# Decode attention beside a gated Mish layer: V and its weights in one load, w1 in K's rows, another closing

## The chip, the cores and the metric

The kernel runs on one core of a Trainium2 chip. The metric is the device time of one execution in microseconds; the kernel before took 220.31 us, the median of 3 runs (220.21 to 220.89). Everything is float32.

## The reference

Two tokens (B = 2, one per batch element) go through two branches, which a gate mixes: attention over the last 4096 positions of a cache, with 32 query heads on 8 key heads, and a dense layer with Mish between two matrices.

```
g = sigmoid((x * gate_w).sum(-1, keepdims=True))          # x: 2 x 1 x 512
q = (x @ wq)                                              # 32 heads of 128
k, v = k_cache[:, :, Sk - W:, :], v_cache[:, :, Sk - W:, :]   # 8 heads, W = 4096, each used by 4 query heads
a = softmax(q k^T * Dh ** -0.5) v @ wo                    # 4096 -> 512
h = x @ w1 + b1                                           # 512 -> 1792
b = (h * tanh(softplus(h))) @ w2                          # 1792 -> 512
out = g * a + (1 - g) * b
```

## The kernel before

The program makes eight turns, one for each key head. In a turn it scores the queries of that head (both batch elements) against 4096 keys each, takes the softmax, multiplies with V, and adds the part of `wo` that belongs to the head before. Beside it, seven of the turns do two of the 14 blocks of 128 rows of the dense layer: `w1`'s pair is multiplied on VectorE, the Mish is worked out on GpSimd and ScalarE, and the result is multiplied with `w2`'s pair one turn later. Both branches add up in one PSUM tile, `acc`. The last head's part of `wo` is added behind the loop, in the tile `fin`.

**Memory.** There is one slot for K and one for V, with no second buffer. `kslot` holds K of a head (8192 numbers in each of 128 partitions) and behind it the next turn's piece of `wq` (2048). `vslot` holds V (8192), `w2`'s pair (1024) and `wo`'s part (2048). `w1s` (L48) holds all seven pairs of `w1`, 1024 numbers each, and a row of zeros for the eighth turn; one load fills it at the start. The host lays out all the arrays so that each partition's row is contiguous.

**The order of the loads.** All loads are issued by SyncE in one queue, in the order of L111 to L140. Ahead of each stands a wait for what frees the slot. K's next load (L120) waits for `qz`, which VectorE gives with the copy of the next queries (L288), behind the maximum of the scores (L329). That copy comes behind the eight products with `wq` (L325), which read the same slot. V is loaded in two halves: the first (L126) waits for `sV`, given when PE has done half of the products with V (L244); the second (L133, with `w2` and `wo` in its rows) waits for `sP`, given behind PE's last product of a turn (L260). The last turn's K, V and weights come in smaller pieces (L123, L135 to L140), so that the work at the end can follow them closely.

**PE in a turn** (L224 to L262): scores (L233), transposition of the maximum (L239), sum of the exponentials (L240), products with V (L244), `w2`'s products with the Mish of the turn before (L253), the transposition of the head's output (L257, which waits for `osel`, the end of a chain on VectorE from L342 to L344), `wo`'s products with the output of the turn before (L260), then `sP`.

**VectorE in a turn** (L322 to L348): the products with `wq` (L325), the maximum (L329), the queries' copy (L288), the bias (L333), the transposition of the probabilities (L335), the copy of `w1`'s pair into `w1c` (L336), products and sums of the dense layer (L292, L298), then the selection of the output (L342 to L344) and its copy into `wst2` (L347).

**The closing** (L264 to L280, L351 to L355): `fin` is filled by five steps of `last`, four with `wo`'s blocks and one that folds `acc`. A step multiplies a 128x32 block with two halves of 256 columns; steps named 0 write the PSUM partitions 0 to 63, those named 1 write 64 to 127. ScalarE copies the upper half to `fs` (L220), VectorE adds the lower half to it (L351), and four rows of 256 numbers are stored (L355).

Of the kernel before, what the change touches and what calls it, by code (L numbers as in the profile page):

```python
# [30 lines left out]
L = 16  # L31

AHEAD = L * (HKV - 1)
NP = PAIRS - 1


def decode_kernel(nc, xg, wq0, w1, kw, k7a, k7b, k7c, va, vb0, vb, v7b, v7c, w26, wo6, wo7a, wo7b, wo7c, out):
    T, V, A, G, SP = nc.tensor, nc.vector, nc.scalar, nc.gpsimd, nc.sync

    def sb(name, n, p=P):  # L40
        return nc.alloc_sbuf_tensor(name, [p, n], F32).ap()

    def ps(name, n):
        return nc.alloc_psum_tensor(name, [P, n], F32).ap()

    kslot = sb("kslot", CHUNK + WQH)
    ks, wqs = kslot[:, :CHUNK], kslot[:, CHUNK:]
    w1s = sb("w1s", HKV * W1P)  # L48
    w1c = sb("w1c", W1P)
    vslot = sb("vslot", CHUNK + 2 * D + WQH + 2 * HKV)  # L50
    vs, w2s, wos = vslot[:, :CHUNK], vslot[:, CHUNK : CHUNK + 2 * D], vslot[:, CHUNK + 2 * D : CHUNK + 2 * D + WQH]
# [6 lines left out]
    b16, qz, wst, hst = (zeros[:, sum(widths[:i]) : sum(widths[: i + 1])] for i in range(len(widths)))  # L58
# [4 lines left out]
    fold = sb("fold", Q)  # L63
# [24 lines left out]
    pq = sb("pq", 8)  # L88
# [2 lines left out]
    md = sb("md", 4)  # L91
    mr = sb("mr", 4)
    accs = sb("accs", D)
    fs = sb("fs", 256, 64)
    res = sb("res", 256, 64)

    acc = ps("acc", D)
    sc = ps("sc", 512)
# [3 lines left out]
    fin = ps("fin", 512)  # L102
    lp = small[:, 0:1]
    ol = small[:, 8:16]

    names = ("ld_x ld_q ld_k ld_kb ld_kc ld_v ld_vb ld_vc ld_w ld_h ld_o ld_w0 ld_w1 ld_w2 c_id c_m c_z c_xb c_eg c_g c_mg "
             "gx g0 g1 g2 g3 g4 g5 hs vx q8 rcp os1 os2 os3 qz mx sA sB bias ex pT sC osel sD sP sE sV wst pq mkr w1c w1p hx hq hd hr accs pe fs res st").split()
    sem = {n: nc.alloc_semaphore(n) for n in names}


# [3 lines left out]
    h = CHUNK // 4  # L114
    parts = ((0, 2 * h), (2 * h, 3 * h), (3 * h, 4 * h))
    for i in range(HKV):
        if i:
            SP.wait_ge(sem["qz"], i + 1)
        if i < PAIRS:
            SP.dma_start(kslot, kw[i]).then_inc(sem["ld_k"], L)  # L120
        else:
            for n, (f, t), src in zip(("ld_k", "ld_kb", "ld_kc"), parts, (k7a, k7b, k7c)):
                SP.dma_start(ks[:, f:t], src).then_inc(sem[n], L)  # L123
        if i:
            SP.wait_ge(sem["sV"], i)
        SP.dma_start(vs[:, : 2 * h], va[i]).then_inc(sem["ld_v"], L)  # L126
        if i:
            SP.wait_ge(sem["sP"], i)
        if i == 0:
            SP.dma_start(vs[:, 2 * h :], vb0).then_inc(sem["ld_vb"], L)  # L130
            SP.dma_start(w1s[:, : PAIRS * W1P], w1).then_inc(sem["ld_w"], L)
        elif i < PAIRS:
            SP.dma_start(vslot[:, 2 * h : CHUNK + 2 * D + WQH], vb[i - 1]).then_inc(sem["ld_vb"], L)  # L133
        else:
            SP.dma_start(vs[:, 2 * h : 3 * h], v7b).then_inc(sem["ld_vb"], L)  # L135
            SP.dma_start(vs[:, 3 * h :], v7c).then_inc(sem["ld_vc"], L)
            SP.dma_start(w2s, w26).then_inc(sem["ld_h"], L)  # L137
# [16 lines left out]
    G.memset(zeros, 0.0).then_inc(sem["c_z"], 1)  # L154
    G.memset(wst2, 0.0)
    G.memset(w2s, 0.0).then_inc(sem["hs"], 1)
    G.memset(w1s[:, PAIRS * W1P :], 0.0).then_inc(sem["ld_w"], L)
    G.wait_ge(sem["c_id"], 1)
    done(G.tensor_tensor(f2, ident[:, : 2 * Q], ident[:, 2 * Q :], op=ALU.add))
    done(G.tensor_tensor(fold, f2[:, :Q], f2[:, Q:], op=ALU.add))  # L160
# [6 lines left out]
    for n in range(NH):  # L167
        i = G.tensor_copy(same.rearrange("p (j y n h) -> p j y n h", j=NJ, n=NH, h=REP)[:, :, :, n, :],
                          key.rearrange("p (y h) -> p y h", h=REP)[:, None].to_broadcast([P, NJ, 4, REP]))
# [35 lines left out]
                        omg[:, None, :].to_broadcast([P, 2, B]), op=ALU.mult).then_inc(sem["hs"], 1)  # L205


    for n in ("ld_kb", "ld_kc", "ld_vc", "ld_o", "ld_h"):
        A.sem_inc(sem[n], AHEAD)
    A.wait_ge(sem["c_eg"], 1)  # L210
    A.activation(eg, zg, AF.Exp, scale=-1.0).then_inc(sem["c_eg"], 1)
# [4 lines left out]
        A.activation(pq, pq, AF.Exp).then_inc(sem["hq"], 1)  # L216
    A.wait_ge(sem["sP"], HKV)
    A.copy(accs, acc).then_inc(sem["accs"], 1)
    A.wait_ge(sem["pe"], 1)
    A.copy(fs, fin[64:, :256]).then_inc(sem["fs"], 1)  # L220


    key_rhs = same[:, :16].rearrange("p (b n h) -> p b n h", b=B, n=NH)[:, :, 0, :]
    with T.Fori(1, HKV + 1, 1) as r:  # L224
        loads = T.lower_val(r * L)

        def after(i, name):
            return i.wait_op(sem[name], loads if name.startswith("ld_") else T.lower_val(r), "sem-ge")

        T.wait_ge(sem["ld_k"], loads)  # L230
        for m in range(BN):
            for j in range(NJ):
                i = T.matmul(sc[Q * j : Q * j + Q, :], qz[:, m * Q : m * Q + Q],  # L233
                             ks[:, (m * NJ + j) * 512 : (m * NJ + j + 1) * 512],
                             start=(m == 0), stop=(m == BN - 1))
                if j == 0 and m != 1:
                    after(i, ("qz", "", "ld_kb", "ld_kc")[m])
        i.then_inc(sem["sA"], 1)
        after(T.transpose(mb[:, :P], mx.to_broadcast([P, P]), ident), "mx").then_inc(sem["sB"], 1)  # L239
        after(T.matmul(lp, same, lsum, start=True, stop=True), "ex").then_inc(sem["sC"], 1)  # L240
        T.wait_ge(sem["ld_v"], loads)
        for c in range(NC):
            j = c % NJ
            i = T.matmul(o[Q * j : Q * j + Q, :], pT[:, c * Q : c * Q + Q], vs[:, c * 512 : c * 512 + 512],  # L244
                         start=(c < NJ), stop=(c >= NC - NJ))
            if j == 0 and c != NJ:
                after(i, ("pT", "", "ld_vb", "ld_vc")[c // NJ])
            if c == NC // 2 - 1:
                i.then_inc(sem["sV"], 1)
        i.then_inc(sem["sD"], 1)  # L250
        T.wait_ge(sem["ld_h"], loads)
        for j in range(2):
            i = T.matmul(acc[Q * j : Q * j + Q, :], hst[:, j * Q : j * Q + Q], w2s[:, j * D : j * D + D],  # L253
                         start=False, stop=False, skip_group_check=True)
            if j == 0:
                after(i, "hs")
        after(T.matmul(ol, osel, key_rhs, start=True, stop=True), "osel").then_inc(sem["sE"], 1)  # L257
        T.wait_ge(sem["ld_o"], loads)
        for j in range(REP):
            i = T.matmul(acc[Q * j : Q * j + Q, :], wst[:, j * Q : j * Q + Q], wos[:, j * D : j * D + D],  # L260
                         start=False, stop=False, skip_group_check=True)
        i.then_inc(sem["sP"], 1)  # L262

    def last(s, lhs, rhs, wait=None, **kw):  # L264
        for u in range(2):
            a = Q * (2 * s + u)
            i = T.matmul(fin[a : a + Q, :256], lhs, rhs[:, u * 256 : u * 256 + 256], skip_group_check=True, **kw)  # L267
# [48 lines left out]
    with V.Fori(1, HKV + 1, 1) as r:  # L316
# [6 lines left out]
        for h in range(REP):  # L323
            for b in range(B):
                i = V.tensor_tensor_reduce(out=junk[:, (h * B + b) * D : (h * B + b) * D + D], in0=wqs[:, h * D : h * D + D],  # L325
                                           in1=xb[b], op0=ALU.mult, op1=ALU.add, scale=1.0, scalar=0.0,
                                           accum_out=q8[:, b * REP + h : b * REP + h + 1])
        i.then_inc(sem["q8"], 1)
        after(V.tensor_reduce(mx, sc, axis=AX.X, op=ALU.max), "sA").then_inc(sem["mx"], 1)  # L329
        after(queries_out(), "q8")  # L330
        V.wait_ge(sem["c_m"], 1)
# [1 line left out]
        V.tensor_tensor_reduce(out=junkb, in0=mb[:, :P], in1=mask, op0=ALU.add, op1=ALU.min, scale=-SCALE,  # L333
                               scalar=BIG, accum_out=bias).then_inc(sem["bias"], 1)
        after(V.transpose(pT, prob), "ex").then_inc(sem["pT"], 1)  # L335
        at(V.tensor_copy(w1c, w1s[:, bass.ds((r - 1) * W1P, W1P)]), "ld_w", 2 * L).then_inc(sem["w1c"], 1)  # L336
# [10 lines left out]
        after(V.tensor_copy(wst2v, ol.rearrange("p (b h) -> p h b", b=B)), "sE").then_inc(sem["wst"], 1)  # L347
# [3 lines left out]
    at(V.tensor_tensor(res, fin[:64, :256], fs, op=ALU.add), "pe", 2).then_inc(sem["res"], 1)  # L351
# [3 lines left out]
    SP.dma_start(out, res[:: Q // B, :]).then_inc(sem["st"], L)  # L355
    SP.wait_ge(sem["hs"], HKV + 1)
    SP.wait_ge(sem["st"], L)
    nums = sorted(s.num for s in sem.values())
# [46 lines left out]
```

## Time and profile before

| what | value |
|---|---|
| median of 3 runs | 220.31 us (220.21 to 220.89) |
| the profiled execution, its own time | 220.1 us |
| its span, first to last instruction | 218.8 us |
| busy: PE, VectorE, ScalarE, GpSimd | 118.8, 126.2, 10.3, 26.2 us |
| bytes read from HBM | 91.26 MB |
| mean granted clock of TensorE | 0.797 |

The profile is that of one execution. Engines are PE (matmul), PEld (its weight loads), DVE (VectorE), ACT (ScalarE), POOL (GpSimd) and SP (SyncE); SPq is SP's queue of DMA issues. Rows of the sequence views give the start in us from the span's start, the duration in us, the engine, the line, the operation and, in brackets, the idle time before it and what ended it. Rows of groups end with the busy us and the mean ns of one, then the idle time before them. In the list of DMA issues, the last number is the time from issue to landing, the median where there are several. In the chain of waits a DMA's row begins at its issue and ends when it has landed.

### The profile page before, as it was taken

The page shows a single profiled execution, that of the slowest core. Times are in us where ns is not written, and L with a number is a line of the kernel's source. Part 1 is how long each engine was busy: PE and PEld are TensorE (multiplying, and loading weights), DVE is VectorE, ACT ScalarE, POOL GpSimd, SP SyncE. Part 2 cuts the span into 40 slices and gives each one's busy share as a digit, 9 for nine tenths or more (in the row PEclk, how much of TensorE's full clock was granted, in tenths as well). Part 3 has the DMA queues.
Part 4 walks back from the last instruction along what each step waited for, and adds up shares of the span by engine and source line. Part 5 has one row for each costly group of instructions (what it writes and reads, how often), then busy time and mean ns, then how long its engine had stood idle before and what let it go on. Part 6 is the DMA issues. An engine that isn't in the chain of part 4 may idle for free.

```text
span 218.8 us, 1985 instructions
## 1 busy us (share of the span) xinstructions
PE 118.8 (54%) x668; PEld 31.1 (14%) x668; DVE 126.2 (58%) x268; ACT 10.3 (5%) x28; POOL 26.2 (12%) x118
## 2 busy tenths in 40 slices
PE   0006386058463477807547195924648175984775
PEld 0002021012110112202111022101112022120211
DVE  2897913919743468507673177714693075967850
ACT  2000010000100001000100001000100001000101
POOL 8200000220021000310012000210002100050030
PEclk9999958757969675875988757695996958599599
DMA  8898999989999999989999899999999899999993
GB/s 310 367 479 371 453 446 407 479 377 429 451 434 442 401 437 455 464 374 452 435 407 479 377 429 446 439 442 401 437 455 464 374 446 440 392 412 442 412 410 118
DMA packets 4926, 91.29 MB, mean 417 GB/s; under 512 B 552, under 2 KB 572, under 8 KB 1084
## 3 DMA queue, kind: packets, MB, share of 16 engines
q1 hardware_dynamic: 4924, 91.26, 97.8%
q8 instruction: 1, 0.02, 0.0%
q14 instruction: 1, 0.01, 0.0%
HBM read 91.26 MB, written 0.00 MB: 417 GB/s over the span
## 4 chain that ended last, share of the span: by engine, by line
DMA 73%; PE 15%; DVE 8%; SPq 2%; issue 1%; DVEq 0%
DMA vslot<-in_vb 51%; DMA w1s<-in_w 15%; PE o L244 9%; DMA wol<-in_wo7a 8%; PE acc L260 4%; DVE osc L344 3%; PE small L257 1%; DVE osc L342 1%; DVE junk L292 1%; DVE hxt L298 1%; PE fin L267 1%; SPq L113 0%; DVE w1c L336 0%; DVE xs L300 0%; SPq L137 0%
## 5 line engine op out<-in xcount | busy, mean ns | idle before, releaser
L233 PE MATMUL sc<-kslot,zeros 128*32 128x512 f32 x256 | 42.7, 823 | 51.5 <-DMA kslot<-in_kw 50.2
L325 DVE CUSTOM_DVE_ANT_0 junk<-kslot,xs 128x512 f32<-128x512 f32 x64 | 39.8, 686 | 37.4 <-DMA kslot<-in_kw 36.4
L244 PE MATMUL o<-vslot,pT 128*32 128x512 f32 x256 | 48.2, 897 | 12.8 <-DMA vslot<-in_vb 10.1
L233 PEld LDWEIGHTS sc<-kslot,zeros 128*32 128x32 f32 x256 | 10.7, 145 | 83.2 <-issue 80.4
L187 POOL TENSOR_TENSOR hb<-hxt,zeros 128x4 f32<-128x4 f32 x8 | 1.7, 216 | 147.0 <-DVE hxt L298 147.0
L292 DVE TENSOR_TENSOR junk<-w1c,xs 128x2048 f32<-128x2048 f32 x8 | 18.3, 2293 | 0.3
L298 DVE TENSOR_REDUCE hxt<-junk 128x4 f32<-128x2048 f32 x8 | 18.3, 2286 | 0.3
L244 PEld LDWEIGHTS o<-vslot,pT 128*32 128x32 f32 x256 | 9.2, 147 | 42.4 <-issue 19.1
L342 DVE TENSOR_SCALAR osc<-o,mkr 128x128 f32<-128x128 f32 x8 | 2.8, 351 | 15.1 <-PE o L244 15.1
L214 ACT ACTIVATE prob<-sc,bias 128x512 f32<-128x512 f32 x8 | 5.5, 687 | 118.7 <-DVE bias L333 118.7
L257 PE MATMUL small<-same,osc 128*128 128x8 f32 x16 | 3.3, 280 | 12.7 <-DVE osc L344 12.7
L240 PE MATMUL small<-lsum,same 128*128 128x1 f32 x16 | 4.1, 324 | 10.5 <-ACT prob L214 10.5
L260 PE MATMUL acc<-vslot,zeros 128*32 128x512 f32 x64 | 9.4, 662 | 0.6 <-DMA vslot<-in_wo 0.6
L335 DVE STREAM_TRANSPOSE pT<-prob 128x512 f32<-128x512 f32 x8 | 5.7, 712 | 6.8 <-ACT prob L214 6.8
L336 DVE COPY w1c<-w1s 128x1024 f32 x8 | 5.2, 656 | 7.5 <-DMA w1s<-in_w 7.5
L344 DVE SCALAR_TENSOR_TENSOR osc<-o,mkr,osc 128x128 f32<-128x128 f32 x24 | 8.4, 351 | 0.9
L253 PE MATMUL acc<-vslot,zeros 128*32 128x512 f32 x32 | 8.6, 616 | 0.3 <-DMA vslot<-in_w 0.3
L329 DVE TENSOR_REDUCE mx<-sc 128x1 f32<-128x512 f32 x8 | 5.5, 691 | 5.6 <-PE sc L233 5.6
L239 PE MATMUL mb<-ident,mx 128*128 128x128 f32 x8 | 2.6, 322 | 9.1 <-DVE mx L329 9.1
L257 PEld LDWEIGHTS small<-same,osc 128*128 128x128 f32 x16 | 2.6, 203 | 20.2 <-DVE osc L344 20.2
L325 DVE DVE_READ_ACCUMULATOR2_ANT q<- 128x1 f32 x64 | 5.2, 81 | 0.0
L240 PEld LDWEIGHTS small<-lsum,same 128*128 128x128 f32 x16 | 3.4, 265 | 12.0 <-ACT prob L214 12.0
(63 smaller groups left out, 64.8 us busy)
## 6 DMA issues: line engine op xcount, KB each, us to landing
kslot<-in_kw SPq DMA_DIRECT2D x7, 5120.0 KB, 19.3
vslot<-in_vb SPq DMA_DIRECT2D x6, 3584.0 KB, 18.9
vslot<-in_va SPq DMA_DIRECT2D x8, 2048.0 KB, 19.9
w1s<-in_w SPq DMA_DIRECT2D x1, 3584.0 KB, 32.7
vslot<-in_vb SPq DMA_DIRECT2D x1, 2048.0 KB, 24.6
kslot<-in_k7a SPq DMA_DIRECT2D x1, 2048.0 KB, 11.1
vslot<-in_wq SPq DMA_DIRECT2D x1, 1031.0 KB, 5.2
kslot<-in_k7b SPq DMA_DIRECT2D x1, 1024.0 KB, 13.2
```

The lines of the kernel that those rows point to most:

```text
L214: A.activation(prob, sc, AF.Exp, bias=bias, scale=SCALE, accum_out=lsum).then_inc(sem["ex"], 1)
L233: i = T.matmul(sc[Q * j : Q * j + Q, :], qz[:, m * Q : m * Q + Q], ks[:, (m * NJ + j) * 512 : (m * NJ + j + 1) * 512], start=(m == 0), sto ...
L240: after(T.matmul(lp, same, lsum, start=True, stop=True), "ex").then_inc(sem["sC"], 1)
L244: i = T.matmul(o[Q * j : Q * j + Q, :], pT[:, c * Q : c * Q + Q], vs[:, c * 512 : c * 512 + 512], start=(c < NJ), stop=(c >= NC - NJ))
L253: i = T.matmul(acc[Q * j : Q * j + Q, :], hst[:, j * Q : j * Q + Q], w2s[:, j * D : j * D + D], start=False, stop=False, skip_group_check= ...
L257: after(T.matmul(ol, osel, key_rhs, start=True, stop=True), "osel").then_inc(sem["sE"], 1)
L260: i = T.matmul(acc[Q * j : Q * j + Q, :], wst[:, j * Q : j * Q + Q], wos[:, j * D : j * D + D], start=False, stop=False, skip_group_check= ...
L292: return V.tensor_tensor(out.rearrange("p (b c d) -> p b c d", b=B, c=n), lhs.rearrange("p (c d) -> p c d", c=n)[:, None, :, :].to_broadca ...
L298: return V.tensor_reduce(out, junk[:, : n * D].rearrange("p (c d) -> p c d", d=D), axis=AX.X, op=ALU.add)
L325: i = V.tensor_tensor_reduce(out=junk[:, (h * B + b) * D : (h * B + b) * D + D], in0=wqs[:, h * D : h * D + D], in1=xb[b], op0=ALU.mult, o ...
L335: after(V.transpose(pT, prob), "ex").then_inc(sem["pT"], 1)
L344: after(V.scalar_tensor_tensor(osc[:, m * DH : m * DH + DH], o[:, m * DH : m * DH + DH], mkr[:, m : m + 1], osc[:, m * DH - DH : m * DH], ...
```

## The change

- V of turns 0 to 6 is one load. In turn 0 it is V alone; in turns 1 to 6 its rows hold V, `w2` and `wo`, and it waits for `sP` alone. The last turn's V keeps its pieces and its waits for `sV` and `sP`.
- `w1` has no load of its own: each pair rides behind K and `wq` in `kslot`'s rows. `w1s` shrinks to one pair, GpSimd's memset of the row of zeros goes, and VectorE's copy into `w1c` moves up, between the products with `wq` and the maximum.
- PE gives `sP` ahead of the transposition of the head's output: `wo`'s products are done first, the transposition after.
- In the closing, a step of `last` multiplies with four pieces of 128 columns, one for each group of 32 PSUM partitions, and all five steps add to the same place. VectorE copies the result from PSUM, ScalarE's copy and the addition go, and eight rows of 128 numbers are stored.

```
-    kslot = sb("kslot", CHUNK + WQH)
-    ks, wqs = kslot[:, :CHUNK], kslot[:, CHUNK:]
-    w1s = sb("w1s", HKV * W1P)
+    kslot = sb("kslot", CHUNK + WQH + W1P)
+    ks, wqs, w1s = kslot[:, :CHUNK], kslot[:, CHUNK : CHUNK + WQH], kslot[:, CHUNK + WQH :]
...
-    fs = sb("fs", 256, 64)
-    res = sb("res", 256, 64)
+    res = sb("res", P)
...
-        if i:
+        if i == 0:
+            SP.dma_start(vs, v0).then_inc(sem["ld_v"], L)
+        elif i < PAIRS:
+            SP.wait_ge(sem["sP"], i)
+            SP.dma_start(vslot[:, : CHUNK + 2 * D + WQH], vw[i - 1]).then_inc(sem["ld_v"], L)
+        else:
             SP.wait_ge(sem["sV"], i)
-        SP.dma_start(vs[:, : 2 * h], va[i]).then_inc(sem["ld_v"], L)
-        if i:
+            SP.dma_start(vs[:, : 2 * h], v7a).then_inc(sem["ld_v"], L)
             SP.wait_ge(sem["sP"], i)
-        if i == 0:
-            SP.dma_start(vs[:, 2 * h :], vb0).then_inc(sem["ld_vb"], L)
-            SP.dma_start(w1s[:, : PAIRS * W1P], w1).then_inc(sem["ld_w"], L)
-        elif i < PAIRS:
-            SP.dma_start(vslot[:, 2 * h : CHUNK + 2 * D + WQH], vb[i - 1]).then_inc(sem["ld_vb"], L)
-        else:
             SP.dma_start(vs[:, 2 * h : 3 * h], v7b).then_inc(sem["ld_vb"], L)
...
-    G.memset(w1s[:, PAIRS * W1P :], 0.0).then_inc(sem["ld_w"], L)
...
-    for n in ("ld_kb", "ld_kc", "ld_vc", "ld_o", "ld_h"):
+    for n in ("ld_kb", "ld_kc", "ld_vb", "ld_vc", "ld_o", "ld_h"):
         A.sem_inc(sem[n], AHEAD)
...
-    A.wait_ge(sem["pe"], 1)
-    A.copy(fs, fin[64:, :256]).then_inc(sem["fs"], 1)
...
-        after(T.matmul(ol, osel, key_rhs, start=True, stop=True), "osel").then_inc(sem["sE"], 1)
         T.wait_ge(sem["ld_o"], loads)
         for j in range(REP):
             i = T.matmul(acc[Q * j : Q * j + Q, :], wst[:, j * Q : j * Q + Q], wos[:, j * D : j * D + D],
                          start=False, stop=False, skip_group_check=True)
         i.then_inc(sem["sP"], 1)
-
-    def last(s, lhs, rhs, wait=None, **kw):
-        for u in range(2):
-            a = Q * (2 * s + u)
-            i = T.matmul(fin[a : a + Q, :256], lhs, rhs[:, u * 256 : u * 256 + 256], skip_group_check=True, **kw)
+        after(T.matmul(ol, osel, key_rhs, start=True, stop=True), "osel").then_inc(sem["sE"], 1)
+
+    def last(lhs, rhs, wait=None, **kw):
+        for u in range(NJ):
+            i = T.matmul(fin[Q * u : Q * u + Q, :P], lhs, rhs[:, u * P : u * P + P], skip_group_check=True, **kw)
...
-    last(0, *wo(0), (sem["ld_w0"], L), start=True, stop=False)
-    last(1, *wo(1), start=True, stop=False)
-    last(0, fold, accs, (sem["accs"], 1), start=False, stop=False)
-    last(1, *wo(2), (sem["ld_w1"], L), start=False, stop=True).then_inc(sem["pe"], 1)
-    last(0, *wo(3), (sem["ld_w2"], L), start=False, stop=True).then_inc(sem["pe"], 1)
+    last(*wo(0), (sem["ld_w0"], L), start=True, stop=False)
+    last(*wo(1), start=False, stop=False)
+    last(fold, accs, (sem["accs"], 1), start=False, stop=False)
+    last(*wo(2), (sem["ld_w1"], L), start=False, stop=False)
+    last(*wo(3), (sem["ld_w2"], L), start=False, stop=True).then_inc(sem["pe"], 1)
...
         i.then_inc(sem["q8"], 1)
+        V.tensor_copy(w1c, w1s).then_inc(sem["w1c"], 1)
         after(V.tensor_reduce(mx, sc, axis=AX.X, op=ALU.max), "sA").then_inc(sem["mx"], 1)
...
-        at(V.tensor_copy(w1c, w1s[:, bass.ds((r - 1) * W1P, W1P)]), "ld_w", 2 * L).then_inc(sem["w1c"], 1)
...
-    V.wait_ge(sem["fs"], 1)
-    at(V.tensor_tensor(res, fin[:64, :256], fs, op=ALU.add), "pe", 2).then_inc(sem["res"], 1)
+    at(V.tensor_copy(res, fin[:, :P]), "pe", 1).then_inc(sem["res"], 1)
...
-    SP.dma_start(out, res[:: Q // B, :]).then_inc(sem["st"], L)
+    SP.dma_start(out.rearrange("b u x -> u b x"), res[:: Q // B, :]).then_inc(sem["st"], L)
...
-        "w1": w1.transpose(1, 0, 2).reshape(P, PAIRS * W1P),
-        "kw": np.concatenate([k[:PAIRS], wq[1:]], axis=2),
+        "kw": np.concatenate([k[:PAIRS], wq[1:], w1], axis=2),
...
-        "va": v[:, :, : 2 * h],
-        "vb0": v[0, :, 2 * h :],
-        "vb": np.concatenate([v[1:PAIRS, :, 2 * h :], w2[:NP], wo[:NP]], axis=2),
+        "v0": v[0],
+        "vw": np.concatenate([v[1:PAIRS], w2[:NP], wo[:NP]], axis=2),
```

More of the change, by code (lines that the diff above doesn't have):

```diff
@@ L34, with decode_kernel @@
 NP = PAIRS - 1
-def decode_kernel(nc, xg, wq0, w1, kw, k7a, k7b, k7c, va, vb0, vb, v7b, v7c, w26, wo6, wo7a, wo7b, wo7c, out):
+def decode_kernel(nc, xg, wq0, kw, k7a, k7b, k7c, v0, vw, v7a, v7b, v7c, w26, wo6, wo7a, wo7b, wo7c, out):
     T, V, A, G, SP = nc.tensor, nc.vector, nc.scalar, nc.gpsimd, nc.sync
@@ L104, in decode_kernel @@
     ol = small[:, 8:16]
-    names = ("ld_x ld_q ld_k ld_kb ld_kc ld_v ld_vb ld_vc ld_w ld_h ld_o ld_w0 ld_w1 ld_w2 c_id c_m c_z c_xb c_eg c_g c_mg "
-             "gx g0 g1 g2 g3 g4 g5 hs vx q8 rcp os1 os2 os3 qz mx sA sB bias ex pT sC osel sD sP sE sV wst pq mkr w1c w1p hx hq hd hr accs pe fs res st").split()
+    names = ("ld_x ld_q ld_k ld_kb ld_kc ld_v ld_vb ld_vc ld_h ld_o ld_w0 ld_w1 ld_w2 c_id c_m c_z c_xb c_eg c_g c_mg "
+             "gx g0 g1 g2 g3 g4 g5 hs vx q8 rcp os1 os2 os3 qz mx sA sB bias ex pT sC osel sD sP sE sV wst pq mkr w1c w1p hx hq hd hr accs pe res st").split()
     sem = {n: nc.alloc_semaphore(n) for n in names}
@@ L385 @@
         "wq0": np.concatenate([wq[0], b1], axis=1),
-        "w1": w1.transpose(1, 0, 2).reshape(P, PAIRS * W1P),
-        "kw": np.concatenate([k[:PAIRS], wq[1:]], axis=2),
+        "kw": np.concatenate([k[:PAIRS], wq[1:], w1], axis=2),
         "k7a": k[PAIRS, :, : 2 * h], "k7b": k[PAIRS, :, 2 * h : 3 * h], "k7c": k[PAIRS, :, 3 * h :],
-        "va": v[:, :, : 2 * h],
-        "vb0": v[0, :, 2 * h :],
-        "vb": np.concatenate([v[1:PAIRS, :, 2 * h :], w2[:NP], wo[:NP]], axis=2),
-        "v7b": v[PAIRS, :, 2 * h : 3 * h], "v7c": v[PAIRS, :, 3 * h :],
+        "v0": v[0],
+        "vw": np.concatenate([v[1:PAIRS], w2[:NP], wo[:NP]], axis=2),
+        "v7a": v[PAIRS, :, : 2 * h], "v7b": v[PAIRS, :, 2 * h : 3 * h], "v7c": v[PAIRS, :, 3 * h :],
         "w26": w2[NP], "wo6": wo[NP],
@@ L399 @@
             for n, t in arrays.items()]
-    args.append(nc.dram_tensor("out_0", (2 * B, 256), F32, kind="ExternalOutput").ap())
+    args.append(nc.dram_tensor("out_0", (B, NJ, P), F32, kind="ExternalOutput").ap())
     decode_kernel(nc, *args)
     r = run_bass_kernel_spmd(nc, [{f"in_{n}": t for n, t in arrays.items()}], core_ids=[0])
-    y = r.results[0]["out_0"].reshape(2, B, 256)
-    return c(y.transpose(1, 0, 2)).reshape(B, 1, D)
+    return c(r.results[0]["out_0"]).reshape(B, 1, D)
```

## The prediction

> **What bounds the kernel now.** I read the page's head and its slices first, then the sums over stretches, to see which resource never stops.
>
> ```profile
> span 218.8 us, 1985 instructions
> DMA  8898999989999999989999899999999899999993
> q1 hardware_dynamic: 4924, 91.26, 97.8%
> 27.00:190.00 163.00, 93.75 (x508) 24.47 (x512) 88.76 (x198) 6.70 (x20) 14.25 (x72) 0.75 1.00 431
> ```
>
> The first row is the span; the second is the busy share of the 16 DMA engines by slice, full up to the last slice; the third says that the one hardware queue held them for 97.8% of the span. The fourth is the stretch from 27 to 190 us: PE, PEld, DVE, ACT and POOL busy for 93.75, 24.47, 88.76, 6.70 and 14.25 us of 163, the granted clock 0.75, then the DMA share, 1.00, and 431 GB/s. No engine is full, the DMA engines are. So the kernel is a stream of 91 MB, and a change counts only if it makes the stream cheaper, makes it stop, or alters what follows its last byte.
>
> Next the list of issues with KB and time to landing, the issues in order, and the chain of waits, which gives the landings.
>
> ```profile
> kslot<-in_kw SPq DMA_DIRECT2D x7, 5120.0 KB, 19.3
> vslot<-in_vb SPq DMA_DIRECT2D x6, 3584.0 KB, 18.9
> vslot<-in_va SPq DMA_DIRECT2D x8, 2048.0 KB, 19.9
> vslot<-in_vb SPq DMA_DIRECT2D x1, 2048.0 KB, 24.6
> vslot<-in_wq SPq DMA_DIRECT2D x1, 1031.0 KB, 5.2
> vslot<-in_v7b SPq DMA_DIRECT2D x1, 1024.0 KB, 11.1
> wol<-in_wo7c SPq DMA_DIRECT2D x1, 256.0 KB, 17.3
> 46.24 15.69 DMA vslot<-in_vb
> 170.66 18.92 DMA vslot<-in_vb
> 195.70 0.33 SPq L135 DMA_DIRECT2D vslot<-in_v7b  x1
> 198.45 0.43 SPq L140 DMA_DIRECT2D wol<-in_wo7c  x1
> ```
>
> V's second half lands at 46.24 + 15.69 = 61.93 in turn 1 and at 170.66 + 18.92 = 189.58 in turn 6: five turns of 25.53 us, each with three loads of 5120 + 2048 + 3584 = 10752 KB. In the closing, v7b lands at 195.70 + 11.1 = 206.8 and wo7c, the last load, at 198.45 + 17.3 = 215.75: 8.95 us for six loads of 1024, 512, 1024, 512, 256 and 256 KB, 3584 KB. Three times that is 10752 KB in 18 loads and 26.85 us. So 15 more loads for the same bytes cost 1.32 us, 0.088 us for each load, and a KB costs (25.53 - 0.26) / 10752 = 0.00235 us.
>
> **The change: bytes and loads.** All bytes stay. Eight loads go: w1's own, and one of the two of V in each of turns 0 to 6. By the fit that is 8 x 0.088 = 0.70 us off the stream, all on the path, since nothing else ends later. The bounds are 0 (the price belongs to the closing's short rows and not to a load as such) and 0.7; I take 0.70, because the price comes from a comparison at equal bytes. The Trainium skill ("DMA: Bandwidth & Descriptors", Anatomy of one DMA) puts a fixed cost of about 2.0 us on a DMA; eight in series would by that be 16 us, and the row above says that a queued load costs a twentieth of it.
>
> **The releases in a settled turn.** A turn now loads 5632 KB of K with w1's pair and 5632 KB of V with w2 and wo, 5632 x 0.00235 + 0.09 = 13.3 us each. K's next load is issued by the queries' copy (L288); w1's copy, 656 ns, now stands ahead of the maximum before it.
>
> ```profile
> L336 DVE COPY w1c<-w1s 128x1024 f32 x8 | 5.2, 656 | 7.5 <-DMA w1s<-in_w 7.5
> 48.55 0.69 DVE L325 CUSTOM_DVE_ANT_0 junk<-kslot,xs 128x512 f32<-128x512 f32 x1 [3.96 <-DMA kslot<-in_kw]
> 53.87 0.69 DVE L329 TENSOR_REDUCE mx<-sc 128x1 f32<-128x512 f32 x1 [0.33 <-PE sc L233]
> 54.47 0.17 DVE L288 COPY zeros<-q 128x16 f32<-128x16 f32 x1
> 28.99 6.43 PE L244 MATMUL o<-vslot,pT 128*32 128x512 f32 x32 [0.16 <-DVE pT L335]
> 61.98 3.59 PE L244 MATMUL o<-vslot,pT 128*32 128x512 f32 x16 [3.06 <-DMA vslot<-in_vb]
> 35.25 1.03 PE L253 MATMUL acc<-vslot,zeros 128*32 128x512 f32 x4
> 67.60 1.07 PE L260 MATMUL acc<-vslot,zeros 128*32 128x512 f32 x8
> ```
>
> In turn 1 K's release came 54.64 - 48.5 = 6.1 us after K's landing; the copy adds at most 0.66, 0.33 of it inside the wait for the scores. At 6.8 us V's 13.3 us are only half through, so the copy costs nothing here; the cover is V's transfer.
>
> V's release is the risk. The wait for half of V's products (sV) is gone, and the whole of V waits for the end of the turn (sP). From V's landing: products 6.26 us (28.99 to the next group's 35.25), w2's 1.03, wo's 1.07, 8.4 us with 0.04 for the wait. K's transfer covers 13.3 of them, so V is issued 4.9 us before the queue is empty. Behind SP's wait stands only K's next load, whose own release comes after K has landed, later still. The release moved ahead of the transposition takes the selection (the chain between 65.6 and 67.6, 2 us) off these 8.4; without that, 2.9 us would be left. What is needed is the time from an issue to full flow, and only an idle queue shows it:
>
> ```profile
> 0.74 0.39 SPq L111 DMA_DIRECT2D vslot<-in_wq  x1
> 216.90 0.57 SPq L355 DMA_DIRECT2D out<-res  x1
> SPq L357 <- DMA out<-res: 1.1, 1, 1.1
> ```
>
> The kernel's first load took 5.2 us, of which 1031 KB explain 2.5: 2.7 us to start. The 4 KB store took 0.57 + 1.1 = 1.67 us in all. Both fit in 4.9, so V costs 0 per turn. A rule of the Trainium skill speaks against the change: issue a DMA early and wait on it late ("DMA: Bandwidth & Descriptors", Rules for kernel authors). Here half of V is issued later than before, and by the rows above it stays early enough.
>
> **Turn 0 has less cover.** Its queue ends with V, where w1's 3584 KB stood behind V before.
>
> ```profile
> 3.27 0.43 SPq L130 DMA_DIRECT2D vslot<-in_vb  x1
> 18.24 4.99 PE L233 MATMUL sc<-kslot,zeros 128*32 128x512 f32 x32 [18.24 <-DMA kslot<-in_kw]
> 20.96 0.69 DVE L325 CUSTOM_DVE_ANT_0 junk<-kslot,xs 128x512 f32<-128x512 f32 x1 [0.82 <-POOL omg L177]
> 25.87 0.68 DVE L329 TENSOR_REDUCE mx<-sc 128x1 f32<-128x512 f32 x1
> 26.66 0.33 SPq L120 DMA_DIRECT2D kslot<-in_kw  x1
> ```
>
> V0 landed at 3.27 + 24.6 = 27.87. Now 512 KB of w1 ride ahead of it (+1.20) and one load less (-0.09): 28.98. K0 lands at 18.24 + 1.2 = 19.4, still before DVE, which works on the gate until 20.96, so K1's release moves by the copy alone: 26.66 + 0.58 (0.66 less the 0.07 by which neighbours on DVE overlap) = 27.24. Flow starts between 27.24 + 1.67 = 28.9 and 27.24 + 2.7 = 29.9, against a queue that is empty at 28.98: a stop of 0 to 0.95 us. I take 0.2, near the lower end, since this queue is not idle when the load is issued. The Trainium skill's first-byte latency for this kind of issue is about 0.6 us (the same page, Specifications); by it there would be no stop and the sum would be 0.2 lower; no row of this profile has a load issued so near to the end of its queue.
>
> **The closing.** Rows in order of time:
>
> ```profile
> 212.15 0.39 PE L257 MATMUL small<-same,osc 128*128 128x8 f32 x2 [0.36 <-DVE osc L344]
> 212.57 0.17 DVE L347 COPY wst<-small 128x8 f32<-128x8 f32 x1 [0.48 <-PE small L257]
> 213.15 1.06 PE L260 MATMUL acc<-vslot,zeros 128*32 128x512 f32 x8 [0.61 <-DMA vslot<-in_wo]
> 214.43 0.64 PE L267 MATMUL fin<-wol,wst 128*32 128x256 f32 x8 [0.21 <-DMA wol<-in_wo7a]
> 215.78 0.65 PE fin L267 x4
> 216.46 0.42 DVE L351 TENSOR_TENSOR res<-fin,fs 64x256 f32<-64x256 f32 x1 [3.63 <-PE fin L267]
> L342 DVE TENSOR_SCALAR osc<-o,mkr 128x128 f32<-128x128 f32 x8 | 2.8, 351 | 15.1 <-PE o L244 15.1
> ```
>
> Eight or four products on four or two column groups take 1.06 us at 512 columns and 0.65 at 256, so the groups run side by side, and a step of 256 columns is worth 0.41; four groups at 128 columns should take 0.65 - 0.205 = 0.45. The last step after wo7c's landing thus loses 0.20. The copy of 128x128 from PSUM lies between 0.17 (8 columns) and 0.35 (the 128x128 row): 0.33, which is 0.09 less than the addition. ACT's copy of half of the result goes; it ended beside the last products, so 0. But the transposition now stands behind wo's products: wo6 lands at 213.15 - 0.70 = 212.45, its products end at 213.5, transposition and copy follow by 214.1, and four steps of about 0.25 each (0.45 less the 0.2 that a step's end overlaps the next) end at 215.1 to 215.2, where wo7c lands at 215.05. I charge 0.1. The store has eight rows of 512 B for four of 1 KB; 0, within 0.15 either way. POOL's memset of w1's spare row lay at the start, beside the first loads: 0.
>
> **The sum.** -0.70 + 0.2 - 0.20 + 0.1 - 0.09 = -0.69 us. The profiled execution took 220.1 us around a span of 218.8, 0.2 under the median 220.31. On the median: 219.6.
>
> **The rivals.** *The queue stops in turn 0 for the full start of an idle queue:* 0.95 in place of 0.2 gives 220.35. For it speaks that 1.7 us lie between K1's release and V0's landing; against it that a filled queue need not wake. *The loads had no price:* without the 0.70, 220.3; for it, that 2 KB rows took part in the fit; against it, that in the closing 1024 KB loads too run above the proportional 2.41. *V is released too late:* if the clock is lower in the products that now run in one burst (the half in turn 1 took 3.59, the whole would be 7.2) the 4.9 us become 3.9, and with a start of 2.7 still 1.2 are left; from there each us more stops the queue six times, 1 us past it giving 219.6 + 6 = 225.6, slower. It decides where release and start together exceed 13.3 us. *The closing backs up on PE:* if the steps do not run side by side, five of 0.45 from 214.1 end at 216.35 instead of 215.6, +0.75: 220.35.
>
> **How the numbers follow.** The forecast has 0.57 (219.3 to 219.9 by the bounds of its small terms), the stop in turn 0 0.24, loads without a price 0.08, PE's backlog 0.03, the late release 0.08. A difference of 0.3% is 0.66 us, about what can be told from no change. The forecast lies on that edge: of its 0.57, 0.47 are beyond it. So faster 0.47, same 0.45, slower 0.08. The range 219.2 to 220.5 leaves out the late release and the ends of the small terms.
>
> **What would show it.** The DMA share is 1.00 from 27 to 190 us, the settled turn is 11264 x 0.00235 + 0.18 = 26.65 us, wo7c lands near 215.2, K1 is issued near 27.2 and V1 near 38, the last step takes 0.45 us and the copy 0.33. Wrong: a slice short of full near 29 us, or PE's wait for V growing from turn to turn by more than the bytes.

## The result and the profile after

The change makes the kernel slower: 221.85 us, the median of 12 runs (220.33 to 222.86), against 220.28 us for 12 runs of the kernel before (220.07 to 221.55). The ratio is 1.006 with a 95% interval of 1.0042 to 1.0079. The forecast was 219.6 us, in a range of 219.2 to 220.5.

The scatter belongs to the result: the kernel before stays within a few tenths in nearly all its runs, the changed one spreads over 2.5 us. The profiled execution of the changed kernel took 220.33 us, the fastest of the twelve, so a second profile of it, of 221.88 us, is read beside it. First the page of the fastest, with the stretch from 40 to 190 us and the loads (KB and us to landing):

```profile
span 219.0 us, 2007 instructions
DMA  8899999999999999999999999999999999899993
40.00:190.00 150.00, 78.93 (x440) 23.27 (x440) 80.71 (x185) 5.71 (x17) 11.78 (x60) 0.72 1.00 431
kslot<-in_kw SPq DMA_DIRECT2D x7, 5632.0 KB, 19.4
vslot<-in_vw SPq DMA_DIRECT2D x6, 5632.0 KB, 19.1
wol<-in_wo7c SPq DMA_DIRECT2D x1, 256.0 KB, 16.0
```

The shape is the one of before: the DMA engines full, 431 GB/s in the settled stretch. The chain and the issues of the same profile give the landings:

```profile
2.80 27.19 DMA vslot<-in_v
27.04 0.33 SPq L118 DMA_DIRECT2D kslot<-in_kw  x1
37.17 0.33 SPq L126 DMA_DIRECT2D vslot<-in_vw  x1
43.70 5.30 PE L226 MATMUL sc<-kslot,zeros 128*32 128x512 f32 x32 [6.22 <-DMA kslot<-in_kw]
64.27 19.28 DMA vslot<-in_vw
170.49 19.68 DMA vslot<-in_vw
200.21 0.44 SPq L136 DMA_DIRECT2D wol<-in_wo7c  x1
```

V lands at 83.55 in turn 2 and at 190.17 in turn 6: 106.62 / 4 = 26.65 us for a turn, exactly the forecast. K1 is issued at 27.04 (27.2 foretold) and V1 at 37.17 (38). But V0 lands at 29.99 in place of 28.98, K1 at 43.70 in place of 28.98 + 13.3 = 42.3, and wo7c, the last load, at 200.21 + 16.0 = 216.2 in place of 215.05. All the distance is there by turn 1, and nothing of it is made later. Most of it is older than K1: K0 landed at 20.27 by the trace's record of landings, where 19.4 was foretold. From V0 to K1 this execution lost only 0.3 us by that record.

The same rows of the second profile, of an execution at 221.88 us:

```profile
span 220.6 us, 2007 instructions
27.19 0.33 SPq L118 DMA_DIRECT2D kslot<-in_kw  x1
44.66 6.02 PE L226 MATMUL sc<-kslot,zeros 128*32 128x512 f32 x32 [7.98 <-DMA kslot<-in_kw]
36.37 21.48 DMA vslot<-in_vw
65.95 18.57 DMA vslot<-in_vw
wol<-in_wo7c SPq DMA_DIRECT2D x1, 256.0 KB, 15.3
201.90 0.44 SPq L136 DMA_DIRECT2D wol<-in_wo7c  x1
```

K0 landed at 19.35 here and V0 at 29.06, both as foretold to 0.1 us. K1 lands at 44.66, 2.4 us behind the forecast, and wo7c at 201.90 + 15.3 = 217.2, 1.5 later than in the kernel before although eight loads are gone. V1 lands at 57.85 in the chain.

The trace's record of single DMA packets shows how. A row of 44 KB takes an engine 1.67 us. In the fastest execution six of K1's first packets, all near 29 us, took 1.89 to 2.43 us; in the other, 22 packets between 28.2 and 36.7 us took up to 2.61 us. The 16 engines are not hit alike. Each load leaves 16 records of landing, one for each engine, and it has landed when the last of them has come. In the second profile V0's 16 parts land between 28.59 and 29.06 us, K1's between 42.43 and 44.53: from first landing to first it is 13.8 us, near the 13.3 of the sum, from last to last 15.5. The two ends stay 1.9 to 2.1 us apart until wo7c: an engine that has lost time stays behind until the end, and the others do not take over its work. Below, a packet is called slow when it takes over 80 ns more than the median of its size, the first 12 us of the kernel left out: the kernel before has one such packet, the changed kernel 6 and 32 in its two profiles.

### The profile page after: what moved, and what is told of

Its sections match the earlier page's. It is cut to its first block, busy times and chain, and to the rows that moved or that the text cites. A ratio compares the mean times of both kernels' runs of the same rounds, so it can differ in the third digit from the quotient of the medians.

```text
span 219.0 us, 2007 instructions
## 1 busy us (share of the span) xinstructions
PE 113.3 (52%) x688; PEld 34.2 (16%) x688; DVE 125.0 (57%) x268; ACT 10.0 (5%) x27; POOL 25.1 (11%) x117
## 4 chain that ended last, share of the span: by engine, by line
DMA 72%; PE 25%; SPq 1%; issue 1%; DVE 1%
DMA vslot<-in_vw 52%; PE o L237 18%; DMA vslot<-in_v 12%; DMA vslot<-in_wo 7%; PE acc L252 4%; PE acc L246 3%; PE fin L259 1%; SPq L111 0%; DVE xs L292 0%; SPq L132 0%; SPq L133 0%; SPq L118 0%; PE small L255 0%; SPq L131 0%; DVE res L342 0%
## 5 line engine op out<-in xcount | busy, mean ns | idle before, releaser
L226 PE MATMUL sc<-kslot,zeros 128*32 128x512 f32 x256 | 43.6, 843 | 54.1 <-DMA kslot<-in_kw 53.9
L237 PE MATMUL o<-vslot,pT 128*32 128x512 f32 x256 | 45.1, 869 | 28.8 <-DMA vslot<-in_vw 27.5
L226 PEld LDWEIGHTS sc<-kslot,zeros 128*32 128x32 f32 x256 | 11.2, 148 | 79.5 <-issue 79.3
L237 PEld LDWEIGHTS o<-vslot,pT 128*32 128x32 f32 x256 | 11.3, 153 | 55.8 <-issue 54.3
L252 PE MATMUL acc<-vslot,zeros 128*32 128x512 f32 x64 | 14.2, 599 | 0.3 <-DMA vslot<-in_wo 0.3
L246 PE MATMUL acc<-vslot,zeros 128*32 128x512 f32 x32 | 8.3, 592 | 0.0
L194 POOL TENSOR_TENSOR mn<-mn,mr 128x4 f32<-128x4 f32 x8 | 1.6, 198 | 35.8 <-DVE mr L340 35.8
L321 DVE COPY w1c<-kslot 128x1024 f32<-128x1024 f32 x8 | 5.5, 690 | 0.0
L326 DVE CUSTOM_DVE_ANT_0 junkb<-mb,mask 128x128 f32<-128x128 f32 x8 | 2.3, 292 | 3.7 <-PE mb L232 3.7
## 6 DMA issues: line engine op xcount, KB each, us to landing
kslot<-in_kw SPq DMA_DIRECT2D x7, 5632.0 KB, 19.4
vslot<-in_v SPq DMA_DIRECT2D x1, 4096.0 KB, 27.2
```

What stands on the lines that cost most here:

```text
L321: V.tensor_copy(w1c, w1s).then_inc(sem["w1c"], 1)
```

## The experiments

**Theory A** (formed after the result): a load that is issued too short a time ahead of the queue's end gets a slow start on some DMA engines. **Rivals:** B, the loss comes from the long rows or the kernel's start; T3, V's late release stops the queue in every turn; C, the new closing, with the transposition behind wo's products, costs more than it gives. The expectations of the first four experiments, written earlier, call the short start in turn 0 theory 1, the long rows theory 2 and V's late release theory 3. The lead, below, is the time from a load's issue to when the first of the 16 engines has landed its part of the load ahead. A landing's record comes some 0.4 us behind the end of the engine's last packet; counted to that end, every lead is 0.4 to 0.5 us shorter.

**1. The changed kernel again.** No edit.

> The changed kernel once more, for a second profile and its scatter. Both theories: a median of 221.4 to 222.2 us, with runs from 220.3 to 222.9. Theory 1 (the queue runs dry in turn 0): a profile above 221 us shows packets of K1 that wait, and K1 or V1 landing over 1 us later than in the 220.33 us profile (43.7 and 57.0 us), while everything from turn 2 on takes 26.65 us per turn. Theory 2 (rows of 44 KB run unevenly over the DMA engines): turns 2 to 6 themselves take 26.8 us or more. Theory 3 (V released late): V's issue comes less than 2.7 us ahead of K's landing in some turn.

Measured: 222.2 us (220.52 to 223.6, 12 runs), ratio 1.0076 (1.0046 to 1.0105). K1 landed only 1 us later than in the fastest profile. As theory A has it, the loss begins at K1; but there are 10 slow packets near 66 to 69 and 95 to 98 us as well. V's issues there, 65.95 and 92.93, came 3.1 and 2.9 us ahead of the first engine's landing: V waits for the last engine, while the queue ends with the first, so engines that have drifted apart eat up the lead. T3 is not dead, it follows from the drift.

**2. w1 in its own load**, behind V0; K's rows back to 40 KB and w1's copy to its old place.

```
+            SP.dma_start(w1s[:, : PAIRS * W1P], w1).then_inc(sem["ld_w"], L)
...
-        V.tensor_copy(w1c, w1s).then_inc(sem["w1c"], 1)
...
+        at(V.tensor_copy(w1c, w1s[:, bass.ds((r - 1) * W1P, W1P)]), "ld_w", 2 * L).then_inc(sem["w1c"], 1)
```

> The changed kernel with w1 in its own load behind V0 and w1's copy back behind the transposition of the probabilities; V's one load, the early release and the closing stay. Theory 1 (turn 0): the cover is back, so 219.5 us (220.3 less 7 x 0.088 for the loads and 0.2 for the closing) with a scatter as small as that of the kernel before. Theory 2 (long rows): V's rows are still 44 KB, K's 40 KB as before, so a median above 220.7 us with runs over 1 us apart. Theory 3 (late V): as theory 2, above 220.7 us.

Measured: 220.12 us (219.6 to 221.34, 11 runs; a twelfth, of 223.17 us, is left out here and in the ratio), ratio 0.9997 (0.9979 to 1.0014). The loss of turn 0 is gone, no packet is slow before 71 us, and four runs lie below 219.8; but the scatter is not. Its 14 slow packets begin at 72, 124 and 175 us, where V was issued 3.4, 3.3 and 3.2 us ahead; where it was 4.1 and 4.2 us, none are slow. K's load is 512 KB shorter here, so V has 1.2 us less of a lead than in the changed kernel. My expectation of a small scatter missed that.

**3. V in two loads again**, with both waits, w1 in K's rows.

> The changed kernel with V in two loads and its two waits as before; w1 stays in K's rows, and the closing and the early release stay. Theory 1 (turn 0): the queue still ends with V0, so the loss and the scatter stay: a median of 221.5 to 222.8 us, 0.6 above the changed kernel for seven more loads. Theory 2 (long rows): K's rows of 44 KB remain, half of the loss, 220.9 us or more. Theory 3 (late V): the loss goes, 220.2 us.

Measured: 222.39 us (221.67 to 223.07, 6 runs), ratio 1.0097 (1.0078 to 1.0116), 15 slow packets, all at K1 (28.3 to 29.5 us). So the one load of V and its late release are not the main cause; w1's leaving of the queue's end is.

**4. The closing alone**: the kernel before with the new closing and the early release.

> The kernel before with nothing but the new closing and the release ahead of the transposition; all loads as before. All theories: 220.1 us, 0.2 under the kernel before, with its small scatter. If the closing itself brought the loss, 221 us or more.

Measured: 220.25 us (219.64 to 221.49, 12 runs), ratio 0.9992 (0.9981 to 1.0002). No slow packets. The closing alone does not bring 1.5 us to the median. But the profiled execution is the slowest of the twelve, and its rows show why it can be slow:

```profile
215.56 1.08 PE L265 MATMUL fin<-wol,wst 128*32 128x128 f32 x16 [0.35 <-DVE wst L345]
216.79 1.13 PE L265 MATMUL fin<-wol,wst 128*32 128x128 f32 x16
216.00:218.00 2.00, 1.92 (x36) 1.46 (x28) 0.02 (x1) 0.00 (x0) 0.41 (x3) 0.50 0.04 12
```

The five closing steps run from 215.56 to 217.92 us, at a granted clock of 0.50 (the last row's third number from the right), and end 1.6 us after the last landing, at 216.34. That landing is itself 0.6 later than in the kernel before, and all of this is there when K0 lands (18.83 for 18.10): the start scatters with the old loads too.

**5. and 6. A filler behind V0**, 1536 KB and 512 KB, read by nothing.

```
             SP.dma_start(vs, v0).then_inc(sem["ld_v"], L)
+            SP.dma_start(fill, v0[:, :3072]).then_inc(sem["ld_f"], L)
```

> The changed kernel with one more load of 1536 KB behind V0, into a tile that nothing reads; everything else as in the changed kernel. It adds bytes for 3.7 us and puts the end of turn 0's queue 3.6 us later, so that K1 is issued about 6 us ahead of it. Theory A (a load issued less than about 4 us before the queue's end gets a slow start on some DMA engines, which then lag to the end): the loss in turn 0 goes, a median of 223.3 to 224.2 us, 1.5 to 2.0 above the changed kernel in place of 3.7. Theory B (the loss comes from the long rows or the kernel's start, whatever the lead): 225.5 us or more, 3.7 above.

> The changed kernel with one more load behind V0, of 512 KB in place of 1536 KB: bytes for 1.3 us, and K1 is issued about 3.2 us ahead of the queue's end, between the changed kernel's 2 and the 6 of the larger filler. Theory A with its limit between 3.5 and 4 us: K1's first packets are still slow on some engines, though less, and the median is 222.0 to 222.9 us, with a wide scatter. Had a lead of 2.7 us been enough, as the prediction had it: all engines together, as with the larger filler, 221.1 us.

Measured with 1536 KB: 223.51 us (222.94 to 223.97, 4 runs), ratio 1.0131 (1.011 to 1.0152), and not one slow packet. The filler costs 1536 x 0.00235 + 0.09 = 3.7 us of stream, so the changed kernel without its stop would be at 219.8, and the stop in turn 0 costs 2.0 to 2.4 us against its own medians of 221.85 and 222.2, with some 0.6 us either way by the intervals. With 512 KB: 222.1 us (221.34 to 223.1, 6 runs), 1.0076 (1.0052 to 1.0099), five slow packets at K1: its lead came out at 2.0 us in this profile and not at 3.2, so this is no test of a limit near 3, only of one above 2. Rows of the larger filler:

```profile
27.12 0.33 SPq L119 DMA_DIRECT2D kslot<-in_kw  x1
fill<-in_v SPq DMA_DIRECT2D x1, 1536.0 KB, 29.4
46.13 6.43 PE L228 MATMUL sc<-kslot,zeros 128*32 128x512 f32 x32 [8.35 <-DMA kslot<-in_kw]
wol<-in_wo7c SPq DMA_DIRECT2D x1, 256.0 KB, 14.9
203.76 0.43 SPq L138 DMA_DIRECT2D wol<-in_wo7c  x1
```

The last landing is at 203.76 + 14.9 = 218.66; less 3.70 that is 214.96, where the forecast had 215.05. Eight loads fewer do give 0.7 us when the queue never runs short.

**7. The transposition ahead of wo's products again**, all else as changed: V's release comes later in every turn.

> The changed kernel with the transposition of the output back ahead of wo's products, as in the kernel before; loads and closing steps stay. V's release then waits for VectorE's chain, about 2 us more in each turn. Theory A (lead): V is issued 2 to 3 us ahead of the queue's end in every turn in place of 4 to 5.5, first packets are slow in most of turns 1 to 6, and the median is 223.5 us or more, though the closing gains up to 0.5. Theory B (lead without effect while it is over 2.7 us): 221.5 us, the closing's gain alone.

Measured: 225.94 us (224.87 to 226.52, 5 runs), ratio 1.0228 (1.0204 to 1.0253), 103 slow packets. The stretch from 40 to 190 us and two releases against K's landings:

```profile
40.00:190.00 150.00, 83.44 (x440) 23.58 (x440) 76.18 (x182) 5.72 (x17) 11.87 (x60) 0.69 1.00 424
67.78 0.33 SPq L126 DMA_DIRECT2D vslot<-in_vw  x1
72.06 6.06 PE L226 MATMUL sc<-kslot,zeros 128*32 128x512 f32 x32 [4.34 <-DMA kslot<-in_kw]
95.09 0.33 SPq L126 DMA_DIRECT2D vslot<-in_vw  x1
99.40 6.04 PE L226 MATMUL sc<-kslot,zeros 128*32 128x512 f32 x32 [4.37 <-DMA kslot<-in_kw]
```

V is issued 4.3 us ahead of K's last landing, but 1.8 and 2.5 ahead of the first engine's, and this turn takes 27.3 us (67.78 to 95.09) in place of 26.65. The row holds the trap: the DMA share is still 1.00, as a slow packet counts as busy for as long as it takes; only the 424 GB/s, for 431, tells of it.

**8. K1 in two loads**, the first in rows of 16 KB.

> The changed kernel with turn 1's K in two loads, the first 2048 KB in rows of 16 KB, the rest behind it; everything else stays, K1 is issued 2 us ahead of the queue's end as before. Theory D (what is slow is the first row of each engine, and it scales with the row): slow starts of 0.2 us at most, a median of 220.2 to 220.9 us. Theory E (a fixed time from an issue to full flow, whatever the row): as in the changed kernel, 221.5 to 222.5 us.

Measured: 221.98 us (220.37 to 223.1, 6 runs), ratio 1.0079 (1.0058 to 1.0101). Fifteen of K1's first packets took 0.76 to 1.62 us in place of 0.61. The delay does not shrink with the row: theory E of its expectation, a time from the issue.

**9. The narrow closing steps in the old order**, all loads as before.

> The kernel before with the five closing steps of four times 128 columns and the copy from PSUM alone; order and loads as before. Theory C: 0.3 us under the kernel before (0.2 in the last step, 0.1 in the copy), 220.0 us, and without the cold steps of 2.4 us. If the narrow steps themselves are slow: 220.5 us or more.

Measured: 220.02 us (219.87 to 221.03, 11 runs), ratio 0.9992 (0.9977 to 1.0008). That is 0.3 us under the kernel before, measured beside it at 220.34: the size foretold, but within what can be told from no change.

**10. PE's last turn apart**, with the transposition first there, on the kernel of 2.

> The kernel with w1 in its own load, with PE's last turn alone in the old order (transposition ahead of wo's products); turns 1 to 7 as in the changed kernel. Theory C (the transposition behind wo's products puts all five closing steps behind it, 1.3 to 2.4 us by PE's clock): the closing ends 0.4 to 0.6 us after wo7c's landing in every run, and the median falls by 0.3 to 0.8 to 219.6 to 220.0 us. If the closing only waits for the last load: no change, 220.35 us. By theory A the scatter in the loop stays.

Measured: 221.59 us (221.19 to 221.66, 5 runs), ratio 1.0048 (1.0032 to 1.0065). The closing did as foretold, 0.5 us from the last landing (217.54) to the end of its last step, but the whole is over 1 us slower than in 2, where 219.6 to 220.0 was expected. At 202 us, among the last loads, the packet record has a fetch of 16 KB of code, which took 1.07 us of one engine; in every kernel with one loop for PE it comes after 215 us. One DMA engine is 1.0 us behind the next from 88 us on, after a short lead of V, and only 0.3 behind it when K's last piece lands at 199.84. Between that load and the next, across the fetch, the first and the last engine part from 1.5 to 3.0 us, and at the end the last one is 1.8 us behind the next (217.54 against 215.73). That the fetch did this is read from the two profiles that have it so early, this one and the next, and not tested apart.

**11. to 13. Long leads.** w1 in its own load, w2 in K's rows with its products right behind the scores, V with wo in one load: V's release is earlier and K's load as long as in the changed kernel (its rows hold K, wq and w2; V's hold V and wo). First with PE's last turn apart, then in one loop, then in one loop with the transposition first.

```
+            SP.wait_ge(sem["sW"], i)
...
-            SP.dma_start(kslot, kw[i]).then_inc(sem["ld_k"], L)
...
+            SP.dma_start(kslot, kw[i - 1]).then_inc(sem["ld_k"], L)
...
-            SP.dma_start(vslot[:, : CHUNK + 2 * D + WQH], vw[i - 1]).then_inc(sem["ld_v"], L)
+            SP.dma_start(vslot[:, : CHUNK + WQH], vw[i - 1]).then_inc(sem["ld_v"], L)
```

> A version made for long leads with few loads: w1 in its own load behind V0, w2's pair in K's rows (its products come right behind the scores), V with wo's part in one load, the narrow closing, and in PE's last turn the transposition ahead of wo's products. Seven loads fewer than before. By theory A every load is issued over 5 us ahead of the queue's end, so no slow first packets, a small scatter, and 220.3 - 7 x 0.088 - 0.3 = 219.4 us. If the scatter of the kernel with w1 in its own load had another cause than the lead: 220.3 us or more, with runs over 1 us apart.

> The version with long leads, with PE's eight turns in one loop again, so that PE's program is as short as the changed kernel's and the transposition stands behind wo's products in the last turn too. In the two kernels with PE's last turn apart, the trace has a 16 KB fetch of code among the last loads (at 202 and 205 us, behind the last load in all others) and the DMA engine that makes it lags by over 1 us to the end. Theory F (that fetch is what the two lost): no packet waits in the last turns, the stream ends near 215.2 us, the closing costs 0.3 to 1 us more, a median of 219.5 to 220.1 us with a scatter of 1 us. If the long leads themselves cost (w2's products among the scores, other rows): 221 us or more.

> The version with long leads in one loop, with the transposition back ahead of wo's products in every turn. In the version before it the stream ended at 215.14 us without a slow packet, and 2.34 us passed from the last landing to the end of the closing steps, at a granted clock of 0.50. Theory C (the transposition behind wo's products is what the closing and its scatter cost): the steps for wo7a and wo7b are done before wo7c lands, 0.4 to 0.8 us from the landing to the end, a median of 219.3 to 219.8 us. V's lead falls from 5.9 to about 3.9 us: by theory A just enough while the engines stay together; if it is not, slow first packets of V come back and the median is 220.5 us or more.

With the last turn apart: 221.82 us (221.15 to 222.77, 8 runs), 1.0059 (1.0036 to 1.0081), the code fetch at 204 us again, the last engine 1.3 us behind the next from there (206.51 against 205.22), where all 16 had kept within 0.7 us up to then. In one loop: 220.78 us (219.27 to 222.21, 12 runs), 1.0002 (0.9974 to 1.0031), and no slow packet at all. Both miss their expectations, of 219.4 and of 219.5 to 220.1 us. The last landing and the closing of that execution, of 221.15 us:

```profile
197.48 0.43 SPq L141 DMA_DIRECT2D wol<-in_wo7c  x1
wol<-in_wo7c SPq DMA_DIRECT2D x1, 256.0 KB, 17.6
212.50 1.73 PE L259 MATMUL acc<-vslot,zeros 128*32 128x512 f32 x8 [1.43 <-DMA vslot<-in_wo]
214.16 0.60 PE L262 MATMUL small<-same,osc 128*128 128x8 f32 x2
215.12 1.08 PE L267 MATMUL fin<-wol,wst 128*32 128x128 f32 x16 [0.36 <-DVE wst L347]
216.37 1.11 PE L267 MATMUL fin<-wol,wst 128*32 128x128 f32 x16
216.00:218.00 2.00, 1.48 (x28) 1.03 (x20) 0.29 (x1) 0.00 (x0) 0.04 (x1) 0.50 0.05 12
```

The stream ends at 215.08, 0.67 earlier than before, and here the closing gives it back: wo's products 1.73 us, the five steps from 215.12 to 217.48, 2.4 us after the last landing, at a granted clock of 0.50, as in experiment 4. In the fastest profile of the changed kernel the clock was 1.00 at that place:

```profile
213.72 1.07 PE L252 MATMUL acc<-vslot,zeros 128*32 128x512 f32 x8 [0.29 <-DMA vslot<-in_wo]
214.71 0.39 PE L255 MATMUL small<-same,osc 128*128 128x8 f32 x2
215.46 0.64 PE L259 MATMUL fin<-wol,wst 128*32 128x128 f32 x16 [0.35 <-DVE wst L339]
216.11 0.65 PE L259 MATMUL fin<-wol,wst 128*32 128x128 f32 x16
216.00:218.00 2.00, 0.76 (x28) 0.47 (x20) 0.29 (x1) 0.00 (x0) 0.36 (x2) 1.00 0.05 12
216.81 0.29 DVE L342 COPY res<-fin 128x128 f32<-128x128 f32 x1 [1.42 <-PE fin L259]
```

There the five steps take 1.3 us and end 0.56 after the last landing (216.2). In the old order, as in experiment 9, four of them are done while the last loads are still on the way, and one is left:

```profile
215.89 0.43 PE L265 MATMUL fin<-wol,wst 128*32 128x128 f32 x8 [0.27 <-DMA wol<-in_wo7c]
```

It ends 0.5 us after the last landing. So theory C holds as a mechanism. In the new order the steps end 0.5 to 1.1 us after the last landing where the clock was 1.00 at that place (experiment 2 and both profiles of the changed kernel), and 1.6 and 2.4 us where it was 0.50 (experiment 4 and this one). The old order is no cure by itself: in the first of these three versions wo's products stood behind a transposition that waited for the selection until 214.5, and at a clock of 0.50 the five steps ended at 218.65, 2.3 us after the landing at 216.38. In 4 against 9, one order against the other, the medians differ by 0.2 us, inside both intervals.

The third, with the transposition first, was to have the old closing. Measured: 224.6 us (223.67 to 225.08, 5 runs), 1.0193 (1.0172 to 1.0215), 65 slow packets:

```profile
72.10 0.33 SPq L132 DMA_DIRECT2D vslot<-in_vw  x1
76.95 5.49 PE L232 MATMUL sc<-kslot,zeros 128*32 128x512 f32 x32 [4.91 <-DMA kslot<-in_kw]
98.93 0.33 SPq L132 DMA_DIRECT2D vslot<-in_vw  x1
102.41 6.42 PE L232 MATMUL sc<-kslot,zeros 128*32 128x512 f32 x32 [3.51 <-DMA kslot<-in_kw]
```

V's leads are 2.6, 2.9 and 1.5 us in turns 1 to 3 here, not the 3.9 that I had reckoned from one burst of products at full clock. One line of PE's program, moved, is worth 3.8 us against the version in one loop, and in the changed kernel the same line is worth 4.1 (7): without the early release V in one load does not work.

**The leads together.** Over all the profiles some 150 loads with rows of 28 KB or more have a lead of 3.6 us or more, and only two of them a slow first packet, one each, of 0.18 and 0.12 us over the median. From 3.44 down to 2.9 us there are two to eight for each load but one, which has none, mostly up to 0.9 us over (once 1.76); from 2.6 down to 1.2, up to 23 packets, and up to 2.0 us on one of them. The limit lies near 3.5 us. The changed kernel's K1 had 1.8 and 1.4 us in its two profiles. No version beats the kernel before by more than its interval.

## Why the prediction was wrong

**Bytes and loads: right.** 0.088 us a load and 0.00235 us a KB. Settled turns of 26.65 us as foretold, and streams that never run short end where the sum puts them (214.96 for 215.05 in experiment 5; 215.08 with seven loads fewer, 215.13 by the sum, in the second of the long leads).

**Turn 0: this step failed.** It said: "a stop of 0 to 0.95 us. I take 0.2, near the lower end, since this queue is not idle when the load is issued." Two things were wrong in it. The time from an issue to undisturbed flow was bounded by two rows, 1.67 us for a store of 4 KB and 2.7 for the first load of all; what loads of 3.5 to 5.6 MB needed is about 3.5. And the price was taken as one stop of the whole queue, in which the engines stand still and go on together, where it falls unevenly: in the second profile K1's first landing came 0.5 us late and its last 2.1, and the last engine sets when every later load has landed. Experiment 5 puts the price at 2.0 to 2.4 us in the median. That alone turns -0.69 into a loss. The fastest execution, 220.33 us, lies inside the stated range, but by luck: it paid 0.3 us at K1 and 0.9 ahead of it, which the forecast did not have. The rival "the queue stops in turn 0" had the right place and less than half of the price; the sign that I named for it, a slice short of full near 29 us, did not show: the slice reads 9 in both profiles, as a slow packet counts as busy.

**Settled turns: right with luck.** V's lead was reckoned as 4.9 us and 0 taken. In the fastest profile it was 4.0 to 5.4 and no packet was slow; in the other the engines had drifted apart, two leads fell to 3.1 and 2.9, and ten packets were slow again, though the last engine lost nothing by it. The rival "V is released too late" priced each microsecond at six; experiment 7, 2 us later, cost 4 us over the changed kernel.

**w1's copy, the early release: right.** K1's issue came at 27.04, and without the early release the kernel is at 225.94.

**The closing: right for a full clock only.** A step by itself takes 0.43 us (experiment 9; 0.45 foretold), five in a row 1.30, the backlog is there, and the copy took 0.29 us (0.33 foretold). The forecast read all of it from a profile in which the clock was granted in full at that place. With the transposition behind wo's products five steps depend on it, and at half clock they take 1.1 us more (2.36 for 1.30). The rival "the closing backs up on PE" had 0.03; the scatter of the long-lead version, 219.27 to 222.21 with no slow packets in its profile, and the slowest run of experiment 4 speak for more. That the clock makes all of this scatter is not shown: one execution of each has been seen.

**Left open.** What passes in the 3.5 us between an issue and undisturbed flow, and why some engines pay more than others; it is not the length of the row. The kernel's first K meets the same: it is issued at 2.36 us behind a load that ends near 6, and in all profiles its first packets are slow, which moves the start by up to 1 us from execution to execution (K0's landing at 20.27 and at 19.35 in the two profiles of the changed kernel). The prediction has no term for it.

## What to carry to other kernels

In a stream of loads on one queue, a merged load saves little (0.09 us here) and takes away lead: reckon each load's issue against the landing of the first DMA engine, not of the last, and keep 4 us for loads of several megabytes (the limit here was near 3.5). What looks like an idle extra load at the queue's end, w1 here, may be the cover that the next issue needs. Work that follows the last load should be as short as it can be in dependent PE steps, since the clock at that place is not given.

## What the runs showed of the hardware

- A DMA engine that falls behind stays behind: in the second profile the first and the last landing of a load are 2.1 us apart at K1 and 1.9 at wo7c, the last one. The DMA share of a profile stays at 1.00 meanwhile; GB/s by stretch (424 for 431) and the spread of landings show it.
- A load of 3.5 to 5.6 MB on a filled queue needed about 3.5 us from its issue to the first engine's landing ahead of it to start undisturbed. The Trainium skill's first-byte latency of about 0.6 us ("DMA: Bandwidth & Descriptors", Specifications) would give no stop at all in turn 0; the measured 2.0 to 2.4 us say otherwise.
- A fetch of 16 KB of code took 1.07 us. In the two kernels whose PE program was longer it fell among the last loads, at 202 and 204 us, and from there to the end one DMA engine was 1.1 to 1.8 us behind the next.
